# Widening a few small tiles so that every large tile in SBUF starts on a multiple of 128 bytes

## The chip, the cores and the metric

The kernel runs on one core of one Trainium2 chip. The metric is device time in microseconds (us), the median of three executions; the trace is that of one further, profiled execution.

## What is computed

The reference is a gated linear recurrence (called attention in the code) followed by a gated feed-forward network:

```python
# q, k, v, a_re, a_im: (4, 8, 768, 48) float32
mag = np.sqrt(a_re * a_re + a_im * a_im)
scale = np.minimum(mag, 0.999) / (mag + 1e-06)
a_re_n, a_im_n = (a_re * scale, a_im * scale)
for t in range(S):
    new_re = ar * S_re - ai * S_im          # ar, ai: a_re_n, a_im_n at t
    new_im = ar * S_im + ai * S_re
    S_re, S_im = (new_re + kv, new_im)      # kv: outer product of k and v at t
    y[:, :, t] = np.einsum('bhd,bhde->bhe', q[:, :, t], S_re)
# x = y as (3072, 384); w_gate, w_val: (384, 1536), w_out: (1536, 384), float64
g = x @ w_gate
out = (g * sigmoid(g)) * (x @ w_val) @ w_out
```

## The kernel before

The recurrence is done in chunks of 128 time steps. A *slab* is one batch and one chunk (24 of them); a *group* `g` is two slabs (12 groups). For each group `stage_ops` loads `a_re`, `a_im`, `q` and `k`, forms logarithms and angles on VectorE (DVE) and ScalarE (ACT), and leaves scaled `ks` and `qs`. For each slab `slab_ops` brings these into the transposed tile `T` (from slab 6 on by a DVE transpose and 12 DMAs, line 594), multiplies key by query (`p_ps`, line 614), masks (`sc`, line 620), multiplies by `v` and by the carried state `G` (`p_py`, line 645), and leaves the network's input as a rounded part `xh` and a remainder `xl`.

For each group `ffn_ops` then runs over 12 blocks `f` of 128 hidden units. Step `f1` (line 825, tile `p_gv`) multiplies the weight blocks by `xh` and `xl`: from group 1 on that is 18 matmuls in the type fp32r, each with 128 stationary columns (weights, 512 bytes a partition) and 256 moving columns (`xh` or `xl`, 1024 bytes a partition). ACT and DVE make the gated value (`sg`, lines 831 and 836) and split it into `hh` and `hl`. Step `f2` (line 859, tile `p_po`) is 6 matmuls with `hh` or `hl` stationary and 384 moving columns of the output weights (1536 bytes a partition). Group 0 alone is done in plain float32, where the program has two PE instructions for each matmul; there `f2` reads the output weights as every second 4-byte word, and `p_ps` reads `T` in that way in all slabs.

`weight_ops` and `split_ops` turn the float64 weights into two fp32r halves. The result of block `f` is put into the tile of block `f - 1` (`place(nm, f - 1, F32R)`), so `f1` of block 1 reads tile `ww0` and so on; that of block 0 reads `ww-1`. `range_ops` loads the weights again, 36 loads in all, into one spare tile to check their range (`flags`, lines 773 to 782).

`Planner` fixes one order of all work from costs written in the file; each engine follows its own list and waits on semaphores. All DMAs of the work are issued by SyncE (SP). Tiles come from pools that place them one after the other in a partition, in the order of the calls that make them. In the built program each begins at a multiple of 32 bytes. A tile of 4 bytes a partition, such as `count`, takes 32.

Of the kernel before, what the change touches and what calls it, by code (L numbers as in the profile page):

```python
# [9 lines left out]
F32 = mybir.dt.float32  # L10
F32R = mybir.dt.float32r
U32 = mybir.dt.uint32
I32 = mybir.dt.int32
# [4 lines left out]
B, H, S, D = 4, 8, 768, 48  # L18
DM, DF = 384, 1536
P = 128  # L20
# [168 lines left out]
def quick(ctx, tc, q, k, v, a_re, a_im, w_gate, w_val, w_out, out, count):  # L189
# [3 lines left out]
    const = ctx.enter_context(tc.tile_pool(name="const", bufs=1))  # L193
# [12 lines left out]
    ones = const.tile([P, 1], F32, name="ones")  # L206
    warm = const.tile([P, 1], F32, name="warm")
    NFL = 2 * NGRP + NSLAB + 6 * NF
    flags = const.tile([P, NFL], F32, name="flags")
    good = const.tile([P, NFL], F32, name="good")  # L210
    fl_re, fl_ratio, fl_dec, fl_lo, fl_hi = 0, NGRP + 2, 2 * NGRP, 2 * NGRP + NSLAB, 2 * NGRP + NSLAB + 3 * NF
    G = const.tile([96, B, H, 64], F32, name="G")
    vts = [const.tile([P, H, 64], F32, name=f"vt{i}") for i in range(2)]
# [14 lines left out]
    def weight(nm, f, part):  # L228
# [5 lines left out]
        if nm == "o":  # L234
# [4 lines left out]

    SHAPE = {"xh": ([P, KT, 2 * P], F32R), "xl": ([P, KT, 2 * P], F32R), "sg": ([P, 2 * P], F32),  # L240
             "hh": ([P, 2 * P], F32R), "hl": ([P, 2 * P], F32R), "ost": ([P, DM], F32),
             "sc": ([P, 4, P], F32), "T": ([96, 2, H * P], F32), "dec": ([96, 2 * H], F32),
             "qs": ([P, 2 * H, 96], F32), "ks": ([P, 2 * H, 96], F32)}
    STAGES = ("re", "im", "s1", "s2", "s3", "qt", "kt")
    SPLIT = ("hs1", "ls1", "him", "lim")
# [821 lines left out]
@with_exitstack  # L1067
def tile_kernel(ctx, tc, q, k, v, a_re, a_im, w_gate, w_val, w_out, out):
    nc = tc.nc
    w_gate, w_val, w_out = (w if w.dtype == U32 else w.bitcast(U32) for w in (w_gate, w_val, w_out))  # L1070
    keep = ctx.enter_context(tc.tile_pool(name="keep", bufs=1))
    count = keep.tile([1, 1], I32, name="count")
    quick(tc, q, k, v, a_re, a_im, w_gate, w_val, w_out, out, count)
    fit = nc.values_load(count, min_val=0, max_val=P)
    with tc.If(fit < P):
        general(tc, q, k, v, a_re, a_im, w_gate, w_val, w_out, out)
# [29 lines left out]
```

## Time and profile before

| | |
|---|---|
| Median of 3 executions | 665.87 us (664.74 to 666.44) |
| Profiled execution | 665.5 us, of which 663.8 us is the span of the trace |
| PE (matmul) busy | 625.8 us, 94% of the span |
| DVE busy | 499.9 us, 75% |
| ACT busy | 398.0 us, 60% |
| DMA on the work's queue | 76.43 MB, 55.2% of 16 engines' span |
| Mean granted TensorE clock | 0.993 of full speed |

A matmul's busy time in the trace covers its whole way through the pipeline, so busy times of neighbours overlap; how fast PE works is read from the distance between the starts of matmuls. Idle time of an engine that nobody waits for costs nothing.

### The profile page before, as it was taken

The page shows a single profiled execution, that of the slowest core. Times are in us where ns is not written, and L with a number is a line of the kernel's source. Part 1 is how long each engine was busy: PE and PEld are TensorE (multiplying, and loading weights), DVE is VectorE, ACT ScalarE, POOL GpSimd, SP SyncE. Part 2 cuts the span into 40 slices and gives each one's busy share as a digit, 9 for nine tenths or more (in the row PEclk, how much of TensorE's full clock was granted, in tenths as well). Part 3 has the DMA queues.
Part 4 walks back from the last instruction along what each step waited for, and adds up shares of the span by engine and source line. Part 5 has one row for each costly group of instructions (what it writes and reads, how often), then busy time and mean ns, then how long its engine had stood idle before and what let it go on. Part 6 is the DMA issues. An engine that isn't in the chain of part 4 may idle for free.

```text
span 663.8 us, 15503 instructions
## 1 busy us (share of the span) xinstructions
PE 625.8 (94%) x6306; PEld 584.6 (88%) x6306; DVE 499.9 (75%) x923; ACT 398.0 (60%) x654; POOL 2.9 (0%) x9
## 2 busy tenths in 40 slices
PE   2589999999999899999999999999999999999996
PEld 0277787899898899999999998999999999999995
DVE  8699999989776875986976986966876966643332
ACT  7765249876784675765866765976856835311110
POOL 1000000000000000000000000000000000000000
PEclk9999999999999799999999999999999999999999
DMA  9999602357757656666666657666554640330000
GB/s 167 288 284 292 172 24 52 55 111 100 175 102 130 145 116 138 132 143 130 135 148 138 126 139 143 117 139 130 112 105 72 120 85 13 68 67 1 25 1 29
DMA packets 234932, 77.49 MB, mean 117 GB/s; under 512 B 208859, under 2 KB 230621, under 8 KB 234854
## 3 DMA queue, kind: packets, MB, share of 16 engines
q1 hardware_dynamic: 234854, 76.43, 55.2%
q8 instruction: 51, 0.84, 0.5%
q14 instruction: 27, 0.22, 0.1%
HBM read 57.47 MB, written 4.78 MB: 94 GB/s over the span
## 4 chain that ended last, share of the span: by engine, by line
PE 62%; DVE 18%; DMA 9%; ACT 4%; issue 3%; SPq 2%; DVEq 0%; ACTq 0%
PE p_gv L825 33%; PE p_po L859 17%; PE p_ps L614 5%; PE p_py L645 5%; DMA wo<-in_moe_w_val_dram 2%; DMA re<-in_a_re_dram 2%; PE p_pm L672 2%; DVE xl L728 2%; DVE sg L836 1%; DMA wo<-in_moe_w_out_dram 1%; DVE sc L620 1%; DMA wo<-in_moe_w_gate_dram 1%; DMA dr<-ww 1%; PE p_pm L441 1%; ACT s L346 1%
## 5 line engine op out<-in xcount | busy, mean ns | idle before, releaser
L825 PE MATMUL p_gv<-xh,ww 128*128 128x256 f32 x1596 | 315.1, 293 | 1.7 <-DVE sg L836 1.5
L825 PEld LDWEIGHTS p_gv<-xh,ww 128*128 128x128 f32 x1596 | 259.7, 190 | 10.7 <-DVE sg L836 4.0
L825 PE MATMUL p_gv<-xl,ww 128*128 128x256 f32 x726 | 204.1, 281 | 0.0
L942 ACT ACT_TABLE_LOAD x111 | 142.4, 1283 | 1.9
L825 PEld LDWEIGHTS p_gv<-xl,ww 128*128 128x128 f32 x726 | 137.6, 189 | 0.2 <-issue 0.2
L831 ACT ACTIVATE sg<-p_gv 128x256 f32<-128x256 f32 x144 | 53.9, 382 | 136.4 <-PE p_gv L825 135.6
L859 PE MATMUL p_po<-wo,hh 128*128 128x384 f32 x484 | 126.8, 343 | 0.0
L836 DVE TENSOR_TENSOR sg<-sg,p_gv 128x256 f32<-128x256 f32 x144 | 58.8, 414 | 62.7 <-ACT sg L831 62.7
L859 PEld LDWEIGHTS p_po<-wo,hh 128*128 128x128 f32 x484 | 82.1, 190 | 2.3 <-issue 2.0
L859 PE MATMUL p_po<-wo,hl 128*128 128x384 f32 x242 | 81.6, 337 | 0.0
L291 DVE TENSOR_TENSOR hl<-sg,hh 128x256 fp32r<-128x256 f32 x132 | 54.5, 419 | 6.9 <-ACT hh L295 1.6
L614 PE MATMUL p_ps<-T 96*128 96x128 f32 x384 | 53.2, 279 | 0.0
L614 PEld LDWEIGHTS p_ps<-T 96*128 96x128 f32 x384 | 50.6, 196 | 0.9 <-ACT T L295 0.3
L859 PEld LDWEIGHTS p_po<-wo,hl 128*128 128x128 f32 x242 | 45.6, 188 | 0.0
L777 DVE TENSOR_REDUCE flags<-wo 128x1 f32<-128x384 f32 x36 | 19.8, 550 | 28.5 <-DMA wo<-in_moe_w_val_dram 12.5
L295 ACT CAST hh<-sg 128x256 fp32r<-128x256 f32 x49 | 19.8, 404 | 35.6 <-DVE sg L836 30.5
L346 ACT ACTIVATE s<-s 128x768 f32<-128x768 f32 x44 | 36.6, 842 | 3.9 <-DVE s L291 3.6
L645 PE MATMUL p_py<-sc,vt 128*32 128x128 f32 x768 | 37.2, 273 | 1.2 <-ACT xh L654 0.7
L620 DVE TENSOR_TENSOR sc<-p_ps,tri 128x512 f32<-128x512 f32 x48 | 32.7, 682 | 3.1 <-PE p_ps L614 2.6
L645 PE MATMUL p_py<-T,G 96*32 96x128 f32 x640 | 33.4, 280 | 0.0
L825 PE MATMUL p_gv<-xh,ww-1_412 128*128 128x256 f32 x132 | 27.8, 299 | 3.2 <-ACT xh L654 3.2
L782 ACT ACTIVATE wo<-wo 128x384 f32<-128x384 f32 x36 | 20.2, 561 | 14.2 <-DMA wo<-in_moe_w_gate_dram 6.8
(134 smaller groups left out, 805.2 us busy)
## 6 DMA issues: line engine op xcount, KB each, us to landing
T<-ww SPq DMA_DIRECT2D x216, 64.0 KB, 2.2
wo<-in_moe_w_out_dram SPq DMA_DIRECT2D x24, 384.0 KB, 5.8
ww<-in_moe_w_gate_dram SPq DMA_DIRECT2D x12, 384.0 KB, 5.1
vt<-in_v_dram SPq DMA_DIRECT2D x24, 192.0 KB, 4.5
ww<-in_moe_w_val_dram SPq DMA_DIRECT2D x12, 384.0 KB, 6.4
out_dram<-ost SPq DMA_DIRECT2D x24, 192.0 KB, 2.2
wo<-in_moe_w_gate_dram SPq DMA_DIRECT2D x12, 384.0 KB, 3.6
wo<-in_moe_w_val_dram SPq DMA_DIRECT2D x12, 384.0 KB, 4.1
```

Of the source, the lines that this page charges most:

```text
L291: V[e].tensor_tensor(out=out, in0=a, in1=b, op=op)
L295: nc.scalar.copy(out=out, in_=in_)
L346: nc.scalar.activation(out=of(dst), in_=of(source), func=func, scale=scale, **kw)
L614: nc.tensor.matmul(out=ps[:, hh, :], lhsT=kT(4 * qd + hh), rhs=qT(4 * qd + hh), start=True, stop=True)
L620: nc.vector.tensor_tensor(out=s, in0=at_["ps", f"{n}.{qd}"].rearrange("p (h t) -> p h t", h=4), in1=mask.unsqueeze(1).to_broadcast([P, 4, ...
L645: nc.tensor.matmul(out=o, lhsT=l, rhs=r, start=opens, stop=closes, tile_position=(0, 32 * slot))
L782: nc.scalar.activation(out=high(0), in_=high(1), func=AF.Square, accum_out=flags[:, fl_hi + j:fl_hi + j + 1])
L825: nc.tensor.matmul(out=gv[:, i, :], lhsT=l, rhs=r, start=(m == 0), stop=(m == len(mm) - 1))
L831: nc.scalar.activation(out=new("sg", I), in_=at_["gv", I][:, 0:2 * P], func=AF.Silu)
L836: nc.vector.tensor_tensor(out=sg, in0=sg, in1=at_["gv", I][:, 2 * P:4 * P], op=ALU.mult)
L859: nc.tensor.matmul(out=po, lhsT=l[:, cs], rhs=weight("o", f, part), start=f == 0 and j == 0, stop=f == NF - 1 and j == len(products) - 1)
L942: nc.scalar.preload_act_table_set(op.load)
```

## The change

Four tiles get a row that is a whole multiple of 128 bytes; three of them are then used by a slice of the old width, and `dec` is used by its old columns only.

```diff
@@ quick @@
     NFL = 2 * NGRP + NSLAB + 6 * NF
-    flags = const.tile([P, NFL], F32, name="flags")
-    good = const.tile([P, NFL], F32, name="good")
+    flags = const.tile([P, -(-NFL // 32) * 32], F32, name="flags")[:, 0:NFL]
+    good = const.tile([P, -(-NFL // 32) * 32], F32, name="good")[:, 0:NFL]
@@
-             "sc": ([P, 4, P], F32), "T": ([96, 2, H * P], F32), "dec": ([96, 2 * H], F32),
+             "sc": ([P, 4, P], F32), "T": ([96, 2, H * P], F32), "dec": ([96, 4 * H], F32),
@@ tile_kernel @@
-    count = keep.tile([1, 1], I32, name="count")
+
+    count = keep.tile([1, 32], I32, name="count")[:, 0:1]
```

`NFL` is 120, so `flags` and `good` go from 480 to 512 bytes a partition, `dec` (three buffers) from 64 to 128, `count` from 4 to 128.

The order of instructions, their shapes and their waits are the same on every engine; only line numbers behind the edit move by one. What differs is where tiles begin. In the two built programs, in bytes from the start of a partition:

| tile | begins before | rest to 128 | begins after | rest to 128 |
|---|---|---|---|---|
| `tri` | 16544 | 32 | 16640 | 0 |
| `G` | 18656 | 96 | 18816 | 0 |
| `ww9`, `ww10` (blocks 10, 11) | 30944, 40160 | 96 | 31104, 40320 | 0 |
| `ww0`, `ww1`, `ww2` (blocks 1, 2, 3) | 80096, 89312, 95456 | 96 | 80256, 89472, 95616 | 0 |
| `ww3` to `ww8` (blocks 4 to 9) | 101792 to 189856 | 32 | 102144 to 190208 | 0 |
| `ww-1` (block 0) | 202144 | 32 | 202496 | 0 |
| `xh`, `xl` (two buffers each) | 196000, 199072; 123296, 126368 | 32 | 196352, 199424; 123648, 126720 | 0 |
| `T` | 132512, 140704 | 32 | 132864, 141056 | 0 |
| `hh`, `hl` | 222624 to 225696 | 32 | 222976 to 226048 | 0 |
| `re`, `im`, `s1`, `s2`, `s3`, `qt`, `kt` | 58592 to 77024 | 96 | 58752 to 77184 | 0 |
| `ks`, `qs`, `sc` | 111008 to 169376 | 32 | 111360 to 169728 | 0 |

The tiles `wo`, which `f2` reads, had a rest of 96 in blocks 1, 10 and 11 and of 32 in the other nine; after the change it is 0 in all. The slices that `f1` and `f2` take of all these tiles begin whole multiples of 512 bytes behind the tile's start.

## Rows read from the trace of the kernel before

**Rows 1.** Three stretches; columns: length, busy (count) by engine, clock, DMA share, GB/s.
```profile
core 0: us, PE busy (x) PEld busy (x) DVE busy (x) ACT busy (x) POOL busy (x), PEclk, DMA share, GB/s
105.00:224.00 119.00, 112.08 (x1162) 105.50 (x1163) 101.89 (x181) 86.75 (x142) 0.00 (x0) 0.97 0.57 108
224.00:500.00 276.00, 273.82 (x3033) 263.72 (x3032) 214.09 (x397) 193.62 (x319) 0.00 (x0) 1.00 0.64 132
500.00:664.00 164.00, 157.67 (x1467) 154.16 (x1465) 87.57 (x184) 57.09 (x101) 0.00 (x0) 0.99 0.24 47
```

**Rows 2.** Chain that ended last, shares by line: 105 to 224 us.
```profile
by line: PE p_gv L825 21.9%; PE p_po L859 11.6%; issue 5.9%; DMA im<-in_a_im_dram 5.5%; DMA wo<-in_moe_w_out_dram 4.4%; PE p_ps L614 4.0%; DVE sg L836 3.7%; PE p_py L645 3.3%; DMA wo<-in_moe_w_gate_dram 3.2%; DVE ks L291 3.0%; DMA re<-in_a_
```

**Rows 3.** The same, 224 to 500 us.
```profile
by line: PE p_gv L825 38.0%; PE p_po L859 18.3%; PE p_ps L614 6.1%; PE p_py L645 5.6%; DMA wo<-in_moe_w_val_dram 4.5%; PE p_pm L672 2.4%; SPq L594 2.1%; issue 2.1%; ACT s L346 2.0%; DMA wo<-in_moe_w_gate_dram 1.8%; PE p_pm L441 1.5%; DVE qs
```

**Rows 4.** The same, 500 us to the end (163.9 us).
```profile
by line: PE p_gv L825 54.0%; PE p_po L859 28.3%; PE p_py L645 5.9%; PE p_ps L614 5.7%; PE p_pm L441 1.8%; PE p_pm L672 0.5%; ACT ost L295 0.3%; PE p_pm L892 0.1%; issue 0.0%
```

**Rows 5.** Who waited for whom, PE alone, 224 to 660 us: total, times, longest.
```profile
PE p_gv L825 <- DVE sg L836: 1.1, 3, 0.4
PE p_pm L441 <- DVE s L502: 0.9, 1, 0.9
```

**Rows 6.** The chain in time order, last group, blocks 0 to 11: start, length, what.
```profile
617.08 2.15 PE p_gv L825 x18
619.22 1.04 PE p_po L859 x6
620.27 2.12 PE p_gv L825 x18
...
626.60 2.12 PE p_gv L825 x18
628.72 1.04 PE p_po L859 x6
629.76 2.15 PE p_gv L825 x18
...
645.74 2.15 PE p_gv L825 x18
647.88 1.05 PE p_po L859 x6
648.93 2.12 PE p_gv L825 x18
651.05 1.04 PE p_po L859 x6
652.10 2.12 PE p_gv L825 x18
```

**Rows 7.** One stretch of 4 us, columns as in rows 1.
```profile
219.60:223.60 4.00, 4.00 (x19) 4.00 (x19) 4.00 (x7) 1.18 (x3) 0.00 (x0) 0.50 0.92 209
```

**Rows 8.** PE's timeline in that stretch: start, busy, operation.
```profile
219.61 0.63 PE L825 MATMUL p_gv<-xh,ww-1_412 128*128 128x256 f32 x2
...
222.81 0.41 PE L825 MATMUL p_gv<-xh,ww-1_412 128*128 128x256 f32 x1
223.02 0.84 PE L859 MATMUL p_po<-wo,hh 128*128 128x384 f32 x2
223.66 0.52 PE L859 MATMUL p_po<-wo,hl 128*128 128x384 f32 x1
```

**Rows 9.** PE's timeline in group 0, plain float32.
```profile
70.97 1.51 PE L859 MATMUL p_po<-wo,sg 128*128 128x384 f32 x4
72.32 2.75 PE L825 MATMUL p_gv<-xh,ww 128*128 128x256 f32 x12
74.91 0.50 PE L859 MATMUL p_po<-wo,sg 128*128 128x384 f32 x1
```

**Rows 10.** The chain in time order, one `p_ps`.
```profile
293.08 0.94 PE p_ps L614 x8
```

**Rows 11.** The chain in time order, 224 to 340 us, where it leaves PE.
```profile
242.50 0.38 ACT sg L831
...
264.92 0.62 PE p_pm L441 x2
...
313.43 0.69 DVE sc L620
...
337.23 2.42 PE p_gv L825 x18
```

**Rows 12.** The same, 400 to 470 us.
```profile
402.24 1.28 ACT L942
404.16 3.91 DMA wo<-in_moe_w_val_dram
...
432.67 0.43 DVE sg L836
433.14 2.33 PE p_gv L825 x18
```

**Rows 13.** DVE's timeline, operations back to back: start, busy, operation.
```profile
421.33 0.95 DVE L291 TENSOR_TENSOR qs<-qt,s 128x768 f32<-128x768 f32 x1
422.20 0.95 DVE L291 TENSOR_TENSOR ks<-kt,s 128x768 f32<-128x768 f32 x1
423.07 0.41 DVE L836 TENSOR_TENSOR sg<-sg,p_gv 128x256 f32<-128x256 f32 x1
...
427.12 0.95 DVE L291 TENSOR_TENSOR re<-re,s 128x768 f32<-128x768 f32 x1
427.99 0.95 DVE L291 TENSOR_TENSOR im<-im,s 128x768 f32<-128x768 f32 x1
428.86 0.41 DVE L836 TENSOR_TENSOR sg<-sg,p_gv 128x256 f32<-128x256 f32 x1
```

## The prediction

> **What bounds the kernel now.** I read the chain that ended last first, by stretches. From 500 us on it is PE alone: `p_gv` 54.0%, `p_po` 28.3%, `p_ps` 5.7%, and nothing of DVE [rows 4]. From 224 to 500 us PE still leads, with 38.0, 18.3 and 6.1%, but DMA, ACT and DVE hold pieces of the chain [rows 3]. From 105 to 224 us PE has well under half [rows 2]; before that, in the set-up, it hardly counts. The table of who waited for whom then says how tight PE is: its waits from 224 to 660 us are 1.1 and 0.9 us, in 436 us [rows 5]. Busy times by stretch say what stands behind PE: DVE 214 of 276 us in the middle and 88 of 164 us at the end [rows 1]. So the kernel is as fast as matmuls follow each other, and the question is what the addresses do to that.
>
> The chain in time order gives the pace. In the last group an `f1` of 18 matmuls takes 2.12 or 2.15 us and an `f2` of 6 takes 1.04 [rows 6]: 117.8 or 119.4 ns for 256 moving columns, 173.3 ns for 384. [...] So at full clock each matmul pays 11.1 to 12.7 ns (256) or 13.3 ns (384) that it doesn't pay at half clock.
>
> Three readings say what this extra is. [...] Second, `f1` of blocks 1, 2, 3, 10 and 11 takes 2.12 us, that of blocks 0 and 4 to 9 takes 2.15 us [rows 6]. The shapes are the same; what differs is that the first five have their weights in a `ww` tile with a rest of 96, the other seven in one with a rest of 32. So a start within 128 bytes is felt. Third, the size: at full rate 128 bytes are 32 columns, 13.3 ns. A moving operand of 1024 bytes that starts off a multiple of 128 touches nine pieces of 128 bytes, not eight: 9 x 13.33 = 120.0 ns. With 1536 bytes it is 13 pieces, 173.3 ns; `T` with its 1024 bytes 120.0 ns; group 0's `f2` with 3072 bytes 25 pieces, 333 ns. Measured: 117.8 to 119.4, 173.3, 117.5, 337.5. That PE is fed in such pieces is my inference from these four, not something that a row states, and it doesn't say why the weights' start matters too.
>
> **The change, part by part.** It adds and removes no instruction, no byte and no wait. All `ww`, `wo`, `xh`, `xl`, `hh`, `hl` and `T` go to a rest of 0.
>
> *Matmuls.* The bounds for a 256-column matmul afterwards are the columns alone, 106.7 ns, and today's 119.4. I take the columns plus the 2.5 ns that float32 pays [rows 9], since that stream is fed without a shortage: 109.2 ns, and 162.5 for 384. The mean `f1` today is (5 x 2.12 + 7 x 2.15) / 12 = 2.1375 us and becomes 18 x 109.2 = 1.966, 8.0% less; `f2` goes from 1.04 to 0.975, 6.25% less; `p_ps` from 0.94 to 8 x 109.2 = 0.874, 7.0% less.
>
> On the chain this is: from 500 us on (163.9 us) 88.5 us of `p_gv` x 8.0% = 7.1, 46.4 x 6.25% = 2.9, 9.3 x 7.0% = 0.65, together 10.7 us [rows 4]. Nothing is near: DVE is busy 53%, ACT 35% of the stretch [rows 1]. I take all of it. From 224 to 500 us: 104.9 x 8.0% + 50.5 x 6.25% + 16.8 x 7.0% = 8.4 + 3.2 + 1.2 = 12.8 us [rows 3]. Here the other engines have long lists in fixed order, and three times the chain already runs through them while PE goes on and waits at the end: from 242.50 to 264.92, 313.43 to 337.23 [rows 11] and 402.24 to 433.14 us [rows 12], 77 of 276 us, 28%. What is late next is DVE's `sg`, `s` or `sc`, or a range-check load that blocks DVE (3.91 us in the last of these [rows 12]). I let the shortened chain lose the same share once more: 12.8 x 0.72 = 9.2 us. From 105 to 224 us: 26.1 x 8.0% + 13.8 x 6.25% + 4.8 x 7.0% = 3.3 us, of which I keep PE's share of that chain, 41% [rows 2]: 1.3 us. Before 105 us nothing.
>
> *DVE and ACT.* DVE's operations of 768 columns start 0.87 us apart whether they write `qs` and `ks` (rest 32) or `re` and `im` (rest 96), and those of 256 columns 0.33 us [rows 13]: 0.54 us for 512 columns leaves 0.06 us that doesn't grow with size. If half of that were a price of the start, the 762 operations from 105 us on [rows 1] would lose 23 us of busy time, most of it off the chain; the two rests cost the same, so I take nothing, and keep a few us for the range.
>
> *DMAs.* The same pieces land at other addresses. On the chain of 224 to 500 us the named loads have 6.3%, 17 us [rows 3]; a tenth of it would be 1.7 us. No row prices it; I take nothing, with 0 to 2 us for the range. The wider rows of `dec` leave its 4-byte pieces as they are.
>
> Sum: 10.7 + 9.2 + 1.3 = 21.2 us off the profiled execution's 665.5 (its span is 663.8), 644.3; the median of 665.87 lies 0.4 us above that execution. I say **644 us**.
>
> [...]
>
> **The rivals.** *Part of the extra stays.* If half of it belongs to starting a new operand whatever its address, half of 21.2 us is gained: 655 us. For it: the extra of rest 96 is smaller, so it isn't a clean whole piece.
>
> *None of it goes.* The 11 to 13 ns could be the price of each new operand at full rate, hidden at half rate, and the blocks' 0.03 us a side matter of which weights come where. Then 665.5 us, give or take the measurement. For it: no row has an fp32r matmul with a rest of 0. Against it: the extra is one piece of 128 bytes to within a ns in `f2`, and the start does matter in `f1`. [...]
>
> *Slower: equal starts collide.* In `f1` the moving operand has a rest of 32; the blocks whose weights have 32 too are the slower ones, those with 96 the faster [rows 6]. If weights and moving operand disturb each other when their pieces begin together, the change makes all of them equal. Its least price is 0.03 us in five of twelve `f1` of 11 groups, 55 x 0.03 = 1.7 us, 667 us; if each of the 2376 matmuls of `f1` and 792 of `f2` lost a tenth of a piece more, 3168 x 1.33 ns = 4.2 us, 670 us. It decides from 2 us on, that is 0.6 ns a matmul. Against it: group 0's float32 `f1` has both operands at 32 and pays 2.5 ns [rows 9].
>
> **How the numbers follow.** The forecast has 0.60, half of the extra 0.13, none 0.17, collision 0.07, and 0.03 is for something not thought of, shared between a gain and a loss. A change within 0.3%, 2 us, is about what a measurement can't tell from none. Faster by more: 0.75; within: 0.17; slower: 0.08. The forecast's own range: if the shorter PE time is given back more than I say in the middle, 10 us less, 654; at most all 132 pairs of `f1` and `f2` gain 0.172 + 0.065 us, 48 `p_ps` 0.066 and group 0 some 0.7 us, 35 us, with 2 us of DMA: 629. Half and none reach to 655 and 665.5. I give 631 to 666: nine tenths of the forecast, the half case and most of none.
>
> **What would show it.** Right: `f1` in the last group at 1.97 us in all 12 blocks, `f2` at 0.975, `p_ps` at 0.87; the distance of `f1` starts there 2.95 us and not 3.16 to 3.20; PE's waits from 224 us on grown from 2 to some 6 us, with DVE named. Wrong: `f1` at 2.12 to 2.15 (none), at 2.05 (half), all blocks at 2.15 or more (collision). If the pace is right and the time is not, the middle is where it was lost: PE's waits there would exceed 10 us. If DVE's distances fall below 0.87 us, I mis-sized what I took for nothing.

## The result and the profile after

The changed kernel takes 660.58 us (median of 4 runs, 659.27 to 661.93), the kernel before 665.31 us in the same comparison: a ratio of 0.9927, 95% interval 0.9902 to 0.9952. That is 4.7 us off, inside the range and on the forecast's side, but a fifth of the 21.2 us that the sum gave. Ratios in this document are estimated from all executions of both kernels in one comparison, and can differ by up to 0.2% from the quotient of the medians beside them. The profiled execution has a span of 660.2 us against 663.8.

The matmuls did not become faster. This is the chain in time order in the last group of the changed kernel, blocks 0, 1, 3 and 11, as in [rows 6]: start, length, what.

```profile
613.61 2.15 PE p_gv L825 x18
615.75 1.05 PE p_po L859 x6
616.81 2.15 PE p_gv L825 x18
...
623.22 2.13 PE p_gv L825 x18
...
648.74 2.13 PE p_gv L825 x18
```

`f1` takes 2.13 to 2.15 us where the forecast said 1.97, and `f2` still 1.05. The five blocks that took 2.12 us before (1, 2, 3, 10, 11) have even moved towards 2.15.

What did change is the DMAs. The page's line for the work's queue, whose share was 55.2% before:

```profile
q1 hardware_dynamic: 234854, 76.43, 48.8%
```

Packets and bytes are the same, the time that they took is less. The same by stretches, columns as in [rows 1]; first the kernel after, then the first 40 us of the kernel before, a stretch that [rows 1] leaves out:

```profile
0.00:40.00 40.00, 22.18 (x154) 13.49 (x155) 33.49 (x55) 31.94 (x54) 2.95 (x9) 1.00 1.00 264
...
224.00:500.00 276.00, 273.93 (x3023) 264.18 (x3022) 211.31 (x391) 192.96 (x318) 0.00 (x0) 1.00 0.56 130
```
```profile
0.00:40.00 40.00, 20.07 (x97) 11.57 (x98) 31.36 (x52) 29.84 (x52) 2.95 (x9) 1.00 1.14 245
```

In the set-up the queue moves 264 GB/s and not 245, and PE gets through 154 matmuls there and not 97. From 224 to 500 us the DMA share fell from 0.64 to 0.56 at about the same GB/s. The list of DMA issues names the loads (issues, size, median us from issue to landing); after, then before:

```profile
re<-in_a_re_dram SPq DMA_DIRECT2D x11, 384.0 KB, 4.6
im<-in_a_im_dram SPq DMA_DIRECT2D x11, 384.0 KB, 4.9
```
```profile
re<-in_a_re_dram SPq DMA_DIRECT2D x11, 384.0 KB, 5.1
im<-in_a_im_dram SPq DMA_DIRECT2D x11, 384.0 KB, 5.6
```

Of the other two tiles of the stages, `kt` went from 5.3 to 4.7 us, and `qt` did not get faster (4.7 and 4.8).

On the chain of the first 40 us the first load shrank from 3.12 to 2.78 us, and two round trips through DRAM (`dr`, 4.17 and 4.46 us) no longer end last. After:

```profile
0.82 2.78 DMA ww<-in_a_re_dram
```

Before:

```profile
0.82 3.12 DMA ww<-in_a_re_dram
...
17.80 4.17 DMA dr<-ww
...
28.30 4.46 DMA dr<-ww
```

Since the order on PE is the same in both kernels, one matmul group can serve as a clock mark. The `p_pm` of 48 matmuls near 65 us on PE's timeline, after and then before:

```profile
65.33 0.88 PE L672 MATMUL p_pm<-vt,ks 128*32 128x48 f32 x48
```
```profile
67.45 0.88 PE L672 MATMUL p_pm<-vt,ks 128*32 128x48 f32 x48
```

So 2.1 us are in hand at 65 us; at the same group near 163 us it is still 2.1 (162.70 and 164.80). The next step is at the one long wait of PE behind the set-up, in front of the half-clock stretch of [rows 7, 8]. PE's timeline, with the idle time before the instruction in brackets, after and then before:

```profile
213.45 0.38 PE L825 MATMUL p_gv<-xh,ww-1_412 128*128 128x256 f32 x1 [1.61 <-ACT xh L654]
```
```profile
218.01 0.58 PE L825 MATMUL p_gv<-xh,ww-1_412 128*128 128x256 f32 x1 [3.23 <-ACT xh L654]
```

The lead is 4.6 us there, and 3.4 at the last `f1` (648.74 against 652.10 [rows 6]): 1.2 us are given back on the way. Not all of this lead need be the change's, since the granted clock differs too. In the kernel before, PE's wait of 3.23 us ends in a stretch with a granted clock of 0.50, from 217.2 to 224.1 us; in the kernel after, the wait of 1.61 us is followed by one from 215.0 to 218.4 us. Columns as in [rows 7], after:

```profile
214.60:218.60 4.00, 3.94 (x19) 3.94 (x20) 4.00 (x8) 1.02 (x2) 0.00 (x0) 0.57 0.96 229
```

The stretch is 3.4 us shorter, which at half the clock is at most 1.7 us of PE's time, by estimate. The clock varies between executions of one kernel: its mean is 0.994 to 0.999 in the four timed ones of the kernel after.

PE's waits from 224 us on have not grown, as they answer to [rows 5]:

```profile
PE p_gv L825 <- DVE sg L836: 0.8, 2, 0.5
PE p_pm L441 <- ACT qs L454: 0.6, 1, 0.6
PE p_pm L441 <- DVE s L502: 0.5, 1, 0.5
```

### The profile page after: what moved, and what is told of

Its sections match the earlier page's. It is cut to its first block, busy times and chain, and to the rows that moved or that the text cites. A ratio compares the mean times of both kernels' runs of the same rounds, so it can differ in the third digit from the quotient of the medians.

```text
span 660.2 us, 15503 instructions
## 1 busy us (share of the span) xinstructions
PE 626.5 (95%) x6306; PEld 586.9 (89%) x6306; DVE 500.6 (76%) x923; ACT 398.5 (60%) x654; POOL 3.0 (0%) x9
## 4 chain that ended last, share of the span: by engine, by line
PE 65%; DVE 18%; DMA 7%; ACT 6%; issue 3%; SPq 0%; ACTq 0%; DVEq 0%
PE p_gv L825 34%; PE p_po L859 17%; PE p_ps L614 5%; PE p_py L645 5%; ACT L942 2%; DVE xl L728 2%; ACT s L346 2%; PE p_pm L672 1%; PE p_pm L441 1%; DMA wo<-in_moe_w_val_dram 1%; DVE sg L836 1%; DMA kt<-in_k_dram 1%; DMA wo<-in_moe_w_gate_dram 1%; DVE s L291 1%; DVE ks L291 1%
```

## The experiments

Theory A after this: DMA pieces that start on a multiple of 64 bytes in SBUF are faster, the loads bring the gain, and 128 is not needed. Its rivals: it is the weights, or some other tile behind `dec`, or no address effect at all but a shift. Four kernels with parts of the change were timed against the kernel before.

**A start on 64 bytes only.** With `count` at 64 bytes the tiles ahead of `dec` that DMAs load start on a multiple of 128, those behind on an odd multiple of 64.

```diff
-    count = keep.tile([1, 1], I32, name="count")
+    count = keep.tile([1, 16], I32, name="count")[:, 0:1]
```

> Only count is widened, to 64 bytes. Tiles made before dec (set-up, stage tiles, v, G, ww0 to ww2, ww9 to ww11) then start on a multiple of 128 bytes, those behind dec (T, xh, xl, hh, hl, ww3 to ww8, most wo) 64 bytes past one. Theory A (DMA): pieces of 192 and 256 bytes go faster when their SBUF rows start on a multiple of 64 bytes; the whole gain is there: about 660.6 us, ratio 0.993, first matmul near 10.85 us and PE some 2.1 us earlier than before from 40 us on. Theory B (multiples of 128 are needed): the gain is partial, 662 to 664. Theory C (the gain comes from the matmuls' pace after all): f1 in the last group would have to be shorter than 2.12 to 2.15 us.

Measured: 657.58 against 662.41 us, 0.9932 (0.9911 to 0.9953), and the mark of 67.45 us stands at 64.89. The whole gain is there with half the tiles on odd multiples of 64. The pace of `f1` is that of before, blocks 1, 2, 3, 10 and 11 again at 2.12 us and the others at 2.15; here blocks 9 and 10 on the chain in time order:

```profile
638.21 2.15 PE p_gv L825 x18
...
641.40 2.12 PE p_gv L825 x18
```

**The part ahead of `dec` alone**, with the tiles behind it left on a rest of 32:

```diff
-             "dec": ([96, 2 * H], F32),
+             "dec": ([96, 3 * H], F32),
-    count = keep.tile([1, 1], I32, name="count")
+    count = keep.tile([1, 16], I32, name="count")[:, 0:1]
```

> count is widened to 64 bytes and each dec buffer to 96: tiles before dec start on a multiple of 128, those behind dec keep their rest of 32. Theory A (DMA), with the gain in the loads of the set-up and of the stage tiles: nearly the whole gain, 660.5 to 662 us, with 2.1 us of it in hand at 45 us. If the shuffles into T (behind dec) carry a share, it is less, 662 to 664. Theory C (matmuls): blocks 0 and 4 to 9 of f1 stay at 2.15 us, 1 to 3, 10 and 11 change.

Measured: 657.18 us, 0.9925 (0.9898 to 0.9953), the mark at 64.31 us. **The part behind `dec` alone** is the same `dec` line without the one of `count`:

> Only dec is widened, to 96 bytes a buffer: tiles before dec keep their rest of 96, those behind it (T, xh, xl, hh, hl, ww3 to ww8) start on a multiple of 128. Theory A with the gain in the loads of the set-up: no gain at 45 us, total 664 to 666 us, ratio 0.998 to 1.001. If T or the operands of the matmuls carry the gain, it appears here: 661 to 663.

Measured: 663.15 us, 1.0003 (0.9985 to 1.0021), the mark at 67.53 us:

```profile
67.53 0.88 PE L672 MATMUL p_pm<-vt,ks 128*32 128x48 f32 x48
```

So everything that was gained is gained in the tiles ahead of `dec`: those that the set-up loads into (`ww0` to `ww2`, `ww9` to `ww11` and the `wo` between them), those of the stages, and `vt`. One of them, `wo11`, is also the spare tile of the 36 range-check loads. That `T`, `xh`, `hh` and most weights now start on 128 brought nothing. In both kernels the five blocks take 2.10 us, which no rest explains, since their weights have a rest of 0 in the one and 96 in the other.

The trace of the kernel with the part behind `dec` shows how a profile can mislead: it is as much shorter than that of before (660.1 us against 663.8) as that of the kernel after, although nothing was gained at the mark or in the timed executions. It has no half-clock stretch; columns as in [rows 1], where the clock of these 119 us is 0.97:

```profile
105.00:224.00 119.00, 113.50 (x1191) 107.49 (x1192) 103.74 (x185) 89.29 (x145) 0.00 (x0) 1.00 0.59 111
```

**All tiles 64 bytes further**, which swaps the rests of 96 and 32:

```diff
-    count = keep.tile([1, 1], I32, name="count")
+    count = keep.tile([1, 24], I32, name="count")[:, 0:1]
```

> Only count is widened, to 96 bytes: every tile moves by 64 bytes, so rests of 96 and 32 change places and none is a multiple of 64. Theory A: DMA pieces as slow as before, 665 us, ratio 0.998 to 1.002. If a multiple of 64 is not what the DMAs want, the time could fall here too. For the matmuls: if the rest of the weights' tile sets the pace of f1, blocks 1 to 3, 10 and 11 go from 2.12 to 2.15 us and the other seven from 2.15 to 2.12; if the pace belongs to the blocks for another reason, nothing changes.

Measured: 661.46 us, 0.9987 (0.9967 to 1.0006); `re` and `im` land in 5.1 and 5.7 us and the mark stands at 67.44. Blocks 1, 2, 3, 10 and 11 are still the ones at 2.12 us, though their weights now have the rest of 32. So it is not the rest, and a shift as such brings no gain. A common shift leaves alone the distance by which the weights start behind the moving operand, and the paces of all these kernels sort by it. Modulo 256 bytes it is 64 in the five fast blocks and 0 in the seven others, before and here; in the kernel after it is 128 and 0 (2.13 to 2.15 and 2.14 to 2.15 us), in the two kernels with one part 224 and 0 (2.10 and 2.15). The queue's share is 50.5% in this kernel without a gain, so that share alone is no proof; the mark goes with the gain in all these kernels.

**The loads by themselves.** This kernel computes nothing of the reference: it loads `a_re` and `a_im` in pieces of 192 bytes and the weights in pieces of 1024, six loads to a section, each section at another start in bytes, and shuffles a tile in 12 DMAs as line 594 does.

```diff
+    def rows192(w):
+        for i, t in enumerate(ld):
+            nc.sync.dma_start(out=t[:, w:w + 768].rearrange("p (h d) -> p h d", d=D), ...)
+        for t in ld:
+            look(t, w)          # a copy of one word that waits for the load
+        rows192(0); rows192(8); rows192(16); ...   # starts of 0, 32, 64, ... bytes
```

> A kernel that computes nothing of the reference: loads of 6 tiles of 384 KB in pieces of 192 bytes (as a_re) at starts of 0, 32, 64, 96, 128, 160, 192, 224 and again 0 bytes past a multiple of 256; the same in pieces of 1024 bytes (as the weights) at 0, 32, 64, 128, 0; and the 12 shuffles into T in pieces of 256 bytes with source and destination at (0,0), (32,0), (0,32), (32,32), (96,32), (64,64), (128,0), (0,0). Theory A: 192-byte pieces take the short time at 0, 64, 128, 192 and some 15 to 40% more at 32, 96, 160, 224; shuffles are faster with both at multiples of 64; 1024-byte pieces differ by under 10%. Theory B (128 needed): 64 and 192 are as slow as 32. If the starts don't matter here, the gain in the set-up came from something else.

DVE's timeline shows the landings: each copy starts when its load is there. Starts of 0, 32 and 64 bytes, then 1024-byte pieces at 0 and 32:

```profile
8.12 0.15 DVE L47 COPY junk<-ldc 128x1 uint32<-128x1 uint32 x1 [1.66 <-DMA ldc<-in_a_re_dram]
9.92 0.15 DVE L47 COPY junk<-ldd 128x1 uint32<-128x1 uint32 x1 [1.65 <-DMA ldd<-in_a_im_dram]
...
17.75 0.15 DVE L47 COPY junk<-ldb 128x1 uint32<-128x1 uint32 x1 [1.96 <-DMA ldb<-in_a_im_dram]
19.86 0.15 DVE L47 COPY junk<-ldc 128x1 uint32<-128x1 uint32 x1 [1.96 <-DMA ldc<-in_a_re_dram]
...
29.77 0.15 DVE L47 COPY junk<-ldb 128x1 uint32<-128x1 uint32 x1 [1.66 <-DMA ldb<-in_a_im_dram]
31.57 0.15 DVE L47 COPY junk<-ldc 128x1 uint32<-128x1 uint32 x1 [1.65 <-DMA ldc<-in_a_re_dram]
...
112.64 0.15 DVE L47 COPY junk<-ldd 128x1 uint32<-128x1 uint32 x1 [0.87 <-DMA ldd<-in_moe_w_val_dram]
113.66 0.15 DVE L47 COPY junk<-lde 128x1 uint32<-128x1 uint32 x1 [0.87 <-DMA lde<-in_moe_w_gate_dram]
...
116.98 0.15 DVE L47 COPY junk<-ldb 128x1 uint32<-128x1 uint32 x1 [0.97 <-DMA ldb<-in_moe_w_val_dram]
118.11 0.15 DVE L47 COPY junk<-ldc 128x1 uint32<-128x1 uint32 x1 [0.97 <-DMA ldc<-in_moe_w_gate_dram]
```

A load of 384 KB takes 1.80 us at 0, 2.11 at 32, 1.80 at 64 bytes; 128 and 192 are like 0 (1.81 us), and 96, 160 and 224 like 32 (2.11). That is 17% more for a start off 64. The 1024-byte pieces take 1.02 us at 0 and 1.13 at 32, 64 and 128. The eight shuffles have the rest of the 217.4 us span, some 9.5 us each by estimate; how they differ by start is not shown. For the 192-byte pieces theory A stands, in one execution of this kernel.

**Which loads.** Two kernels split the gain by tile. Both give `re`, `im`, `qt` and `kt` 64 bytes more and start them 32 bytes in; all distances between weights and moving operands stay modulo 256. On the kernel before this puts only these four on a multiple of 64; on the kernel with the 64-byte `count` it takes only these four off it.

```diff
+            if tag in ("re", "im", "qt", "kt"):
+                t = work.tile([P, A2 + 16], dt, name=tag, tag=tag, bufs=slots[tag])[:, 8:8 + A2]
+                t = t.rearrange("p (h d) -> p h d", d=D)
```

> Everything as in the kernel with a 64-byte count, but the loads of the later stages (re, im, qt, kt, 11 each) go to addresses 32 bytes past a multiple of 64; the set-up's tiles and vt start on one. If the gain is made by two parts that add up, the set-up's part is what stood at 65 us in the earlier traces, 2.1 to 3.1 us: ratio 0.995 to 0.997, the large p_pm at 64.3 to 65.4 us, re and im landing in 5.1 and 5.6 us again. If the set-up makes all of it (an early lead that the later waits turn into more): 0.993. If the stages' loads make all of it: 1.000.

> The other half alone: the kernel before, with re, im, qt and kt on multiples of 64 bytes and nothing else moved against the multiples of 64; distances between weights and moving operands stay as before, so f1 stays at 2.12 and 2.15 us. Two parts that add up: ratio 0.996 to 0.998, the large p_pm at 67.4 us as before, re and im landing in 4.6 to 4.9 us. The set-up makes all of it: 1.000. The stages make all of it: 0.993.

Measured: 659.03 against 664.07 us, 0.9906 (0.9882 to 0.9931), for the set-up without the stages; 662.43 us, 0.9962 (0.9938 to 0.9986), for the stages alone. `re` lands in 5.2 and 4.7 us. The mark on PE's timeline, set-up first, then stages:

```profile
65.23 0.88 PE L676 MATMUL p_pm<-vt,ks 128*32 128x48 f32 x48
```
```profile
66.13 0.88 PE L676 MATMUL p_pm<-vt,ks 128*32 128x48 f32 x48
```

The parts do not add up. The set-up's tiles and `vt` alone, expected at 0.995 to 0.997, give all that the change gives. The stages alone give some 2 us (1.6 by the medians, 2.5 by the ratio), inside the 0.996 to 0.998 expected, but 1.3 of it stands at the mark already, where 67.4 had been expected: two of the 11 loads each of `re` and `im` are issued before 65 us, in the set-up. Alone the two have leads of 2.2 and 1.3 us at the mark, together 2.6 in the kernel with the 64-byte `count`. That both shorten the same full queue would explain it; no run shows it by itself. Nor does a run move `vt` or the spare tile of the range-check loads alone, so the set-up's part may hold some of theirs.

**The matmuls by themselves.** Streams of 72 matmuls, nothing of the reference computed, with weights and moving operand at chosen starts.

```diff
+    def stream(bank, W, X, ws, xs, wcols, xcols, n=72):   # ws, xs: first words
+        stream(banks[1], W, X, 0, 0, 128, 256)
+        stream(banks[1], W, X, 16, 0, 128, 256)
...
+        stream(banks[0], BW, BX, 0, 0, 128, 256)
```

> A kernel that computes nothing of the reference: PE alone, streams of 72 matmuls from one set of tiles (18-step pattern of f1), first 24 streams of fp32r 128 stationary by 256 moving columns with the starts of the two operands 0 to 192 and 0 to 96 bytes past a multiple of 256, then streams with fewer stationary columns (96, 64, 32), with 384 and 512 moving columns, in bfloat16, with the same weights again and again, and with starts 4 and 16 bytes off. My prediction's idea (a moving operand off a multiple of 128 bytes is read as one piece more): 109 ns a matmul with the moving operand at 0, 120 at 32, 64 or 96. Rival L (loading 128 columns of 4-byte weights takes reading time from the moving operand): about 118 to 120 ns whatever the starts, and the extra over 106.7 ns shrinks with the stationary columns: 10 ns at 96, 6.7 at 64, 3.3 at 32; in bfloat16 half of it or less. Rival S (a fixed price of starting a new operand at full rate): 118 to 120 ns in all, with 32 stationary columns too.

PE's timeline, one row a stream; the distance of starts divided by 72 is the pace:

```profile
27.27 8.80 PE L60 MATMUL pb<-X,W 128*128 128x256 f32 x72
35.91 8.65 PE L60 MATMUL pc<-X,W 128*128 128x256 f32 x72
...
95.62 8.33 PE L60 MATMUL pb<-X,W 128*128 128x256 f32 x72
103.79 8.68 PE L60 MATMUL pc<-X,W 128*128 128x256 f32 x72
...
247.61 8.32 PE L60 MATMUL pd<-X,W 128*32 128x256 f32 x72
255.77 12.64 PE L60 MATMUL pe<-X,W 128*128 128x384 f32 x72
268.25 12.64 PE L60 MATMUL pf<-X,W 128*64 128x384 f32 x72
...
313.75 8.04 PE L60 MATMUL pa<-BX,BW 128*128 128x256 bf16 x72
321.62 8.02 PE L60 MATMUL pb<-BX,BW 128*128 128x256 bf16 x72
```

With both operands on a multiple of 128 (first row) a matmul takes 8.64 / 72 = 120.0 ns; no start on a multiple of 32 bytes was slower, and only a distance of 160 bytes was as slow (119.9 and 120.0). With the weights 64 bytes past the moving operand (95.62) it takes 113.3 to 113.6, wherever the pair lies; the other distances give 117.2 to 118.8. With 32 stationary columns (247.61) it is 113.3; in bfloat16, with half the bytes, 109.3. 384 columns take 173.3 ns (255.77 to 268.25), which is what `f2` has already. So at none of the starts tried does an fp32r stream of 256 columns run at 109: a start on a multiple of 128 saves nothing, and `f2`'s 173.3 is not 13 pieces, since at a rest of 0, with 12, it is the same. Of the rivals, L comes out with 96 and 64 stationary columns (116.1 and 113.5 ns, against its 116.7 and 113.4) but not with 32 (113.3 against 110.0); S, which had 118 to 120 with 32 columns too, does not come out.

A second such kernel tried more distances and blocks of 18 and 6 matmuls in turn, as `f1` and `f2` follow each other:

```diff
+    def blocks(bank, d1, d2):   # 4 times: 18 as f1, weights d1 words past the moving operand, then 6 as f2 with d2
+        blocks(banks[5], 0, 0); blocks(banks[6], 16, 0); blocks(banks[1], 16, 16)
```

> Computes nothing of the reference: PE alone. Eight streams of 384 moving columns with the weights 0, 32 ... 224 bytes past the moving operand; twelve of 256 columns with distances of 16, 48, 64 and on to 240 bytes; then 4 times 18 matmuls of 256 columns and 6 of 384, with the distances (f1, f2) of (0,0), (64,0), (0,64), (64,32), (64,64), (64,96), (64,128), (64,160), (64,192), (64,224), (128,0), (32,32). Theory E: 384 columns have a fastest distance too (166.7 ns or less, 173.3 at 0), 64 is the fastest for 256 columns and 16 and 48 lie between; a pair of f1 and f2 at (64, best) takes 0.1 us less than 3.2. Rival: 384 columns take 173.3 ns at every distance, and in the alternation f1 is as slow as at 0.

With 384 columns no distance is faster than 0, as the rival had it: 173.3 to 173.5 ns at 0, 32, 96 and 192 bytes, 174.7 to 176.7 at the others. With 256 columns the distance is not all: one of 224 gives 116.7 ns here, with the moving operand on a multiple of 256, and 117.9 in the first kernel, with it 32 to 96 bytes past one. In the alternation four turns take 12.78 us at distances of 0 and 0 bytes, 12.67 at 64 and 0, and 12.34 at 64 and 64. The first turn of the last pair on PE's timeline, and the start of the streams behind its four turns; from start to start `f1` takes 2.06 us:

```profile
281.38 2.22 PE L70 MATMUL pb<-X,W 128*128 128x256 f32 x18
283.44 1.20 PE L74 MATMUL pb<-X,W 128*128 128x384 f32 x6
...
293.72 2.21 PE L70 MATMUL pc<-X,W 128*128 128x256 f32 x18
```

**The distance in the kernel itself.** If the distance counts, `xh` and `xl` should start 64 bytes short of where the weights do, modulo 256, in all blocks. On the kernel after:

```diff
-            t = work.tile(shape, dt, name=tag, tag=tag, bufs=slots[tag])
+            if tag in ("xh", "xl"):
+                t = work.tile([P, KT * 2 * P + 64], dt, name=tag, tag=tag, bufs=slots[tag])[:, 48:48 + KT * 2 * P]
+                t = t.rearrange("p (k n) -> p k n", k=KT)
+            else:
+                t = work.tile(shape, dt, name=tag, tag=tag, bufs=slots[tag] + (tag == "dec"))
```

(`dec` has four buffers of the old width here, so that all large tiles keep one rest.)

> The change with one thing more: all tiles start on a multiple of 64 (the large ones 128 bytes past a multiple of 256), and xh and xl are slices that start 64 bytes less than the weights modulo 256, in all twelve blocks. The computation is whole. Theory E (the streams alone: equal starts of weights and moving operand 120 ns, weights 64 bytes further 113.3): f1 falls from 2.13 to 2.15 us to 2.04 in all blocks, 2376 matmuls x 6 ns = 14 us of PE time, two thirds to all of it on the chain, 647 to 652 us. If f2 between two f1 throws the streams out of step, as in the five blocks of the kernel before that had this distance and took 2.12 us: 2376 x 1.8 ns = 4 us, 656 to 659. Rival (the distance matters in a stream alone only): like the change, 657 to 661 on the chip of the change's timing, ratio 0.993.

Measured: 654.28 against 663.70 us, 0.985 (0.9828 to 0.9873): faster than both kernels, by 0.8% more than the change in its own comparison. Every `f1` of the last group takes 2.04 us on the chain in time order:

```profile
604.82 2.04 PE p_gv L829 x18
606.86 1.05 PE p_po L863 x6
```

The pace is the one that theory E gave, but not the time: 647 to 652 us had been expected of it, and 656 to 659 if `f2` spoils the pace.

With the same distance for `hh` and `hl` too (tiles of `2 * P + 64` words, used from word 16 on):

> As the one before, and hh and hl start 64 bytes past the output weights modulo 256, so f2 has that distance too. The computation is whole. Theory E for f2: 1.04 us falls to 1.00 (166.7 ns a matmul instead of 173.3), 792 x 6.7 = 5 us more of PE time, 643 to 650 us. If the distance does nothing to matmuls of 384 columns: the same as the one before.

Measured: 656.60 us, 0.9897 (0.9863 to 0.9932), and `f1` is at 2.12 us again, `f2` at 1.04:

```profile
603.03 2.12 PE p_gv L831 x18
605.15 1.04 PE p_po L865 x6
```

In pace that is the reverse of the streams, where 64 and 64 was the best pair and 64 and 0 had an `f1` of 2.12 us; the times of the two kernels are not clear of each other (0.9828 to 0.9873 and 0.9863 to 0.9932). Blocks 2 and 3 of the kernel before have the distances 64 and 0 as well, and take 2.12 us. The distance alone doesn't settle which pace a block falls into.

## Why the prediction was wrong

**What bounds the kernel.** Right: PE from 224 us on, and its waits there stayed at 1.9 us (2.0 before). **"Three readings say what this extra is"** is the step that failed, and with it the 109.2 and 162.5 ns that the sum took for a matmul at a rest of 0. They are estimates: half of the 213.3 and 320 ns between starts at a granted clock of 0.50 [rows 7, 8], 106.7 and 160.0, plus the 2.5 ns by which a plain float32 matmul of 256 columns, 215.8 ns [rows 9], exceeds 213.3. No run shows an fp32r matmul at either; the streams at that rest take 120.0 and 173.3 ns. Nor does what is paid above 106.7 go with the rate of bytes alone: it is 2.6 ns in bfloat16, with half the bytes, but in fp32r, at one and the same rate of moving bytes, it is 6.6 with 32 stationary columns and up to 13.3 with 128. The second, that `f1` at 2.12 and 2.15 us shows a start within 128 bytes, was a wrong reading: the two sorts of block differ in their rest and in their distance from `xh`, and swapping the rests left the paces where they were. The third, nine pieces of 13.3 ns, fitted four numbers [rows 6, 9, 10] by chance.

***Matmuls.*** Forecast 10.7 + 9.2 + 1.3 = 21.2 us, measured none: `f1` 2.13 to 2.15, `f2` 1.05, and the `p_ps` matmuls still start 117 to 118 ns apart. *None of it goes* was the right rival for the matmuls, and its reason, that no row had an fp32r matmul with a rest of 0, was the one to weigh more. That the time fell all the same, to within the range, is luck: the gain comes from a term that the sum had at nothing.

***DVE and ACT.*** Nothing, rightly: DVE's 768-column operations on `ks` and `qs`, now at a rest of 0, still start 0.87 us apart:

```profile
416.18 0.95 DVE L291 TENSOR_TENSOR ks<-kt,s 128x768 f32<-128x768 f32 x1
417.05 0.95 DVE L291 TENSOR_TENSOR qs<-qt,s 128x768 f32<-128x768 f32 x1
```

***DMAs.*** Taken at nothing, with 0 to 2 us for the range, and *before 105 us nothing*. This is the mis-sized term: 2.1 us are in hand by 65 us, and the timed gain is 4.7. The prediction looked for the price on the chain from 224 to 500 us; the part that is shown is paid in the first 40 us, where the DMA share is at its highest (1.14 before) and loads and trips through DRAM stand on the chain.

*Equal starts collide* was right in part and small in its price. The change makes the starts equal modulo 128, but modulo 256 the five blocks go from a distance of 64 to one of 128, not to 0; the streams are slowest at 0 and at 160, and the five blocks went from a mean of 2.12 to 2.138 us. 55 of them make 1.0 us, against the 1.7 of its least price. That may be most of the 1.2 us given back after 214 us, but the clock has a hand in that lead too. It did not decide, since the loads gave more.

**What stays open.** Of the 4.7 us, 2.1 are shown at the mark. How the rest comes about is not: in the profile after it is the wait at 213 us, 1.6 us and not 3.2, and the shorter half-clock stretch behind it, but this wait is 2.7 us in the set-up's kernel, which is as fast, and 1.8 in the kernel with the part behind `dec`, which gained nothing. The clock does not make the gain: of the timed executions in the comparison of the 64-byte `count`, those with a mean granted clock of 0.998 and more took 661.3 us in the kernel before (mean of four) and 657.2 in the other (three), those with 0.992 to 0.994 took 664.5 (five) and 661.1 (two): 3.4 to 4.1 us less at like clock. Nor is it settled why fp32r takes 113.3 to 113.6 ns at the best distance and not the 106.7 of the estimate, and why the pair of 64 and 64 is the fastest in the streams and not in the kernel.

## What to carry to other kernels

When rows of 192 bytes are loaded, try tiles that start on a multiple of 64 bytes in SBUF (1.80 and not 2.11 us a load here), first where loads stand on the chain, as in this set-up; a tile of 4 bytes ahead of all others can spoil it for every one. A lead in one pair of traces is no gain by itself: the granted clock can differ between them, as here by 3.4 us at half clock. When two groups of blocks differ in pace, list all that differs in their addresses, the distance between the operands too, and shift everything together before one of these is called the cause. A fit to four durations is no measurement: a stream of 72 matmuls at the new start would have shown that the matmuls had nothing to gain.

## What the runs showed of the hardware

The prediction had neither of two things. A 384-KB load in 192-byte pieces takes 1.80 us when its rows begin on a multiple of 64 bytes and 2.11 us when they begin 32 bytes off, though DRAM and all else are the same. And an fp32r matmul of 256 columns with 128 stationary ones takes between 113.3 and 120.0 ns depending on the distance between where its weights and its moving operand begin, which was worth 0.8% of this kernel, about as much as the change.
